# Attention steps of the next token chunk queued behind a feed-forward unit's last work on every engine

## The chip, the cores and the metric

One NeuronCore of one Trainium2 chip runs the whole program. The metric is device time in microseconds (us) of one execution; lower is better. Matmuls run on TensorE (PE in the rows, PEld its weight loads), elementwise work on VectorE (DVE), ScalarE (ACT) and GpSimd (POOL). All DMAs of this kernel are issued from the queue of SyncE (SP).

## What is computed

The reference runs a gated linear attention and feeds its output through two feed-forward networks:

```python
for t in range(S):                                   # S = 768, B = 4, H = 8, D = 48
    state = alpha[:, :, t, :, None] * state + einsum('bhd,bhe->bhde', k[:, :, t], v[:, :, t])
    y[:, :, t] = einsum('bhd,bhde->bhe', q[:, :, t], state)
x = y.transpose(0, 2, 1, 3).reshape(B * S, H * D)     # 3072 tokens x 384
h = x @ w_in                                          # 384 -> 2048
P = a[0] + a[1]*h + a[2]*h**2 + a[3]*h**3
Q = 1 + |b[0]|*|h| + |b[1]|*h**2
x2 = (P / (Q + 1e-6)) @ w_out                         # 2048 -> 384
h = x2 @ w_in2                                        # 384 -> 1024
out = layernorm(h * softmax(h)) * g_ln @ w_out2       # 1024 -> 384
```

## The kernel before, in words

**Chunks, units, halves.** The 768 time steps are cut into six chunks of 128 steps (4 x 128 = 512 tokens). The first feed-forward network handles a chunk in 16 *units*, one for each 128 columns of the 2048; `u` counts all 96 of them (`c, f = divmod(u, 16)`). A unit's up part, `m_up(u)`, is nine matmuls into the PSUM tile `hp` (L573; three such tiles take turns), then elementwise work on ACT (L578 to L581, L600, L601), DVE (L599, L602 to L604) and POOL, which ends with `fin[u]` (L604 or, for some early units, L597) on DVE, the copy `gh` (L606) on ACT and the remainder `gl` (L607) on POOL. Its down part, `m_down(u)`, is nine matmuls that add `gh` and `gl` into `x2p` (L619); it is written four units after the up part.

**Attention.** A chunk's attention is done in two *halves* (two of the four batches each), so there are 12; half `i` is prepared while the units of the chunk before are at work. `a_pe(i)` has four steps: for each of two groups of heads, `p` = 0 and 1, eight score products `sc` (L416, each recorded as two matmuls), their copies to `A` on ACT (L423) and a causal mask on POOL (L424); then 56 products into `y` (L437, 112 recorded), whose result goes into the next chunk's `xt` (L463 on ACT, L464 on DVE); then 16 products `u` (L474) and the update of the state `Sbd` (L484 on DVE, L485 on POOL, which multiplies by the decay of the whole chunk, `hf.ends`).

**Loading q and k.** `a_prep(i)` makes the scaled q, k and last decay products of a half on DVE and POOL and writes them out to DRAM (`qk_d`, L333; `kb_d`, L325). `a_move(i)`, run at the end of the half before, reads them back in another layout: four DMAs into `qks` (L276), which holds q, k and the last decay products, then v (`vns`, L344) and the k by time (`kns`, L278). `qks` is one buffer for all halves from 2 on, so its new content waits until the old is no longer read.

**What sets the order.** A scheduler orders each engine's instructions at build time, by when it reckons they are ready; at run time each engine takes them strictly in that order. The program can hold an instruction back: inside `with tc.issue_after(ins)` everything traced for the engine of `ins` is placed behind it. For the attention steps this is done by `half_steps`, one step at each unit from `u % 8 == 2` on:

```python
def later(n):
    return tc.issue_after(fin[now[0] - n].ins) if n <= now[0] < GE + n and now[0] - n in fin else ExitStack()
...
with later(GP):            # GP = 2
    a = next(gp, "end")    # a step of a_pe(i)
with later(GS):            # GS = 2
    b = next(gd, "end")    # two steps of a_prep(i + 1), then loads for half i + 2
```

As `fin` is on DVE, only DVE's part of a step is held back; PE, ACT and POOL take theirs where the scheduler reckons them ready.

**Side work.** While u < 16, units share the engines with the preparation of the first network's weights, later (u 16 to some 63) with that of the second's (`split_w`: load `st` L516, three DVE instructions L519 to L523, ACT L529, POOL L530, and a store L532). `judge` (L143) sums flags of a range check. The second network follows from unit 84 on.

Of the kernel before, what the change touches and what calls it, by code (L numbers as in the profile page):

```python
# [7 lines left out]
F32 = mybir.dt.float32  # L8
# [5 lines left out]
ALU = mybir.AluOpType  # L14
# [9 lines left out]
def _run(*gens):  # L24
    for g in gens:
        for _ in g:
            pass
# [3 lines left out]
def kernel(  # L31
# [108 lines left out]

    flag = const.tile([1, 1], I32, name="flag")

    def judge():  # L143

        sums = const.tile([128, 1], F32, name="sums")
        row = const.tile([1, 128], F32, name="row")
        tot = const.tile([1, 1], F32, name="tot")
        nc.vector.tensor_reduce(sums, bad, axis=AX.X, op=ALU.add)
        nc.sync.dma_start(out=row, in_=sums)
        nc.vector.tensor_reduce(tot, row, axis=AX.X, op=ALU.add)  # L150
        nc.vector.tensor_scalar(flag, tot, 0.0, None, ALU.is_gt)

    def network(fast):
# [116 lines left out]
                raws[i, nm] = t  # L270
                yield

        def a_move(i):
            qk, kb = moved.pop(i)
            for m, i0, n, d0 in ((0, 0, 32, 0), (1, 0, 16, 32), (1, 16, 16, 64), (2, 0, 32, 80)):
                nc.sync.dma_start(out=qks[d0:d0 + n], in_=qk[m].rearrange("b i x -> i b x")[i0:i0 + n])  # L276
            v_load(i)
            nc.sync.dma_start(  # L278
                out=kns[:, :B * 192].rearrange("p (b x) -> p b x", b=B), in_=kb[:].rearrange("b t x -> t b x")
            )  # L280
            yield
# [114 lines left out]
        def a_prep(i):  # L396
            if i >= NPE:
                yield from a_dve(i)
# [8 lines left out]
        def a_pe(i):  # L407
            c, bp = divmod(i, 2)
            vt = vts.pop(i)
            hf = half(i)  # L410
            A = {}
            for p in range(2):
                sc = [ps_ap.tile([128, B, CH], F32, name="sc", tag="at") for j in range(2)]
                for x in range(B):
                    for j in range(2):
                        nc.tensor.matmul(  # L416
                            sc[j][:, x, :],
                            lhsT=hf.k[p][64 * j:64 * j + D, x, :], rhs=hf.q[p][64 * j:64 * j + D, x, :],
                            start=True, stop=True,
                        )  # L420
                for j in range(2):
                    t = A[p, j] = ap_.tile([128, B, CH], F32, name="A", tag=f"A{p}{j}")
                    nc.scalar.activation(t, sc[j], AF.Copy)  # L423
                    nc.gpsimd.affine_select(  # L424
                        out=t, in_=t, pattern=[[0, B], [1, CH]], compare_op=ALU.is_ge, fill=0.0, base=0,
                        channel_multiplier=-1,
                    )
                yield

            y2 = [ps_ap.tile([128, n, 2 * CH], F32, name="y", tag="at") for n in (2, 1)]  # L430
            begun = set()

            def put(m, x, w, r, last):
                kt, quad = divmod(m, 4)
                first = (kt // 2, quad) not in begun
                begun.add((kt // 2, quad))
                nc.tensor.matmul(  # L437
                    y2[kt // 2][32 * quad:32 * quad + 32, kt % 2, CH * x:CH * x + CH], lhsT=w, rhs=r,
                    start=first, stop=last, skip_group_check=True,
                )  # L440

            pairs = range(H // 2)
            for x in range(2):
                if c:
                    for hp in pairs:
                        g, p = divmod(hp, 2)
                        for z in range(3):
                            put(
                                3 * hp + z, x, Sbd[:, bp, 2 * (2 * x + g) + p, 32 * z:32 * z + 32],
                                hf.q[p][:, 2 * x + g, :], False,  # L450
                            )
                for part in ((0, 1, 3), (2,)):
                    for hp in pairs:
                        g, p = divmod(hp, 2)
                        for z in part:
                            o = 512 * x + 128 * hp + (0, 32, 48, 80)[z]
                            put(
                                3 * hp + (0, 1, 1, 2)[z], x, vt[:, o:o + 32], A[p, z // 2][:, 2 * x + g, :], z != 1
                            )
            xt = x_tile(c)  # L460
            for z, n in enumerate((2, 1)):
                hi, lo = (xt[:, 2 * z:2 * z + n, w, 256 * bp:256 * bp + 256] for w in range(2))
                nc.scalar.activation(hi, y2[z], AF.Copy)  # L463
                marks[i, z] = nc.vector.tensor_tensor(lo, y2[z], hi.bitcast(F32), ALU.subtract)  # L464
            yield
            if i < NPE:
                a_back(i)
            u = ps_ap.tile([128, B * 2, D], F32, name="u", tag="at")
            for x in range(B):
                for p in range(2):  # L470
                    for j in range(2):
                        o = 192 * x + 96 * p + 48 * j
                        n = 256 * x + 128 * p + 64 * j
                        nc.tensor.matmul(  # L474
                            u[64 * j:64 * j + 64, 2 * x + p, :], lhsT=hf.kn[:, o:o + 64], rhs=vt[:, n:n + D],
                            start=True, stop=True, skip_group_check=True,
                        )
            if c < NCH - 1:
                for j in range(2):
                    rows = slice(64 * j, 64 * j + D)  # L480
                    S = Sbd[rows, bp, :, D * j:D * j + D]
                    S4 = S.rearrange("p (b w) e -> p b w e", b=B)
                    if c:
                        nc.vector.tensor_tensor(S, S, u[rows], ALU.add)  # L484
                        nc.gpsimd.tensor_tensor(S4, S4, hf.ends[rows], ALU.mult)  # L485
                    else:
                        nc.vector.tensor_tensor(
                            S4, u[rows].rearrange("p (b w) e -> p b w e", b=B), hf.ends[rows], ALU.mult
                        )
            yield  # L490

# [68 lines left out]
                )  # L560

        fin = {}
        gts = {}
        x2ps = {}

        def m_up(u):
# [3 lines left out]
            hi, lo = wi[n]  # L570
            for kt in range(KT):
                for w, xx in ((hi, 0), (hi, 1), (lo, 0)):
                    nc.tensor.matmul(  # L573
                        hp, lhsT=w[:, kt, 128 * o:128 * o + 128], rhs=xts[c][:, kt, xx, :],
                        start=(kt == 0 and w is hi and xx == 0), stop=(kt == KT - 1 and w is lo),
                    )
# [26 lines left out]
                nc.vector.scalar_tensor_tensor(hp, w, 2.0, hp, ALU.subtract, ALU.mult, reverse0=True)  # L603
                fin[u] = nc.vector.scalar_tensor_tensor(p, p, a0, hp, ALU.add, ALU.mult)  # L604
            gh, gl = (moe_pool.tile([128, NTOK], F32R, name=nm, tag=nm, bufs=NB[nm]) for nm in ("gh", "gl"))
            nc.scalar.activation(gh, p, AF.Copy)  # L606
            nc.gpsimd.tensor_tensor(gl, p, gh[:].bitcast(F32), ALU.subtract)  # L607
            gts[u] = (gh, gl)

        def m_down(u):  # L610
# [176 lines left out]
        if fast:  # L787
# [16 lines left out]
            _run(a_load(2, ("ra", "rk")))  # L804
            with tc.issue_after(marks[0, 1].ins):
                _run(a_prep(2))
            _run(a_enter(2), pre)
            _run(a_load(3, ("ra", "rk")))
            stage["wide"] = False
# [4 lines left out]
        NH = 2 * NCH  # L814

        now = [0]

        def later(n):
            return tc.issue_after(fin[now[0] - n].ins) if n <= now[0] < GE + n and now[0] - n in fin else ExitStack()

        def half_steps(i):
            gp = a_pe(i)
            gd = chain(a_prep(i + 1), a_load(i + 2, ("ra", "rk")) if i + 2 < NH and i + 1 >= NPE else iter(())) if i + 1 < NH else iter(())
            while True:
                with later(GP):
                    a = next(gp, "end")
                with later(GS):
                    b = next(gd, "end")
                    if b != "end":
                        b = next(gd, "end")  # L830
                if a == "end" and b == "end":
                    if i + 1 < NH:
                        _run(a_enter(i + 1))
                        if i + 2 < NH and i + 1 < NPE:
                            _run(a_load(i + 2))
                    return
                yield

        NU = NCH * NF1
        split2 = w2_split() if fast else iter(())  # L840
        tp = 0.0
        side = iter(())
# [2 lines left out]
        for u in range(NU + LAG):  # L845
# [6 lines left out]
            if u < NU:  # L852
                if f == 0 and c == NCH - 1:
                    if fast:
                        judge()
                    open2()
                    tail = chain(w2_load("i"), n_load(0), w2_load("o"))
                if f == 0 and c and not fast:
# [169 lines left out]
```

## Time and profile before

| | |
|---|---|
| three runs | 814.88, 815.14 and 816.88 us; median 815.14 us |
| the profiled execution | 812.64 us, of which the span from first to last instruction is 810.9 us |
| PE | busy 748.0 us (92%) |
| DVE | busy 634.7 us (78%) |
| ACT, POOL | busy 535.4 us (66%), 361.1 us (45%) |
| mean granted TensorE clock | 0.96 of full speed |

All times of rows are of the profiled execution, counted from the start of its span. In a unit's row of nine matmuls a recorded duration is longer than the distance to the next start, since matmuls overlap; the distances are what counts.

### The profile page before, as it was taken

The page shows a single profiled execution, that of the slowest core. Times are in us where ns is not written, and L with a number is a line of the kernel's source. Part 1 is how long each engine was busy: PE and PEld are TensorE (multiplying, and loading weights), DVE is VectorE, ACT ScalarE, POOL GpSimd, SP SyncE. Part 2 cuts the span into 40 slices and gives each one's busy share as a digit, 9 for nine tenths or more (in the row PEclk, how much of TensorE's full clock was granted, in tenths as well). Part 3 has the DMA queues.
Part 4 walks back from the last instruction along what each step waited for, and adds up shares of the span by engine and source line. Part 5 has one row for each costly group of instructions (what it writes and reads, how often), then busy time and mean ns, then how long its engine had stood idle before and what let it go on. Part 6 is the DMA issues. An engine that isn't in the chain of part 4 may idle for free. (4 is left out here: it accounts for less than half of the span.)

```text
span 810.9 us, 13869 instructions
## 1 busy us (share of the span) xinstructions
PE 748.0 (92%) x4976; PEld 614.9 (76%) x4976; DVE 634.7 (78%) x1110; ACT 535.4 (66%) x983; POOL 361.1 (45%) x294
## 2 busy tenths in 40 slices
PE   4776987999899998999899999999999999999995
PEld 4665776777676775878687777888888989998995
DVE  6996998979698987979798976557877698777720
ACT  2324766777786876687887878798885555555531
POOL 3263778676554453444444433242233514452331
PEclk9857698999999998999999999999999999999999
DMA  7877357355737275355636160460013544552552
GB/s 177 183 186 209 105 122 199 114 138 165 199 93 175 77 235 123 120 118 161 152 99 176 47 150 1 146 244 1 1 39 90 151 95 119 132 117 50 121 129 58
DMA packets 87279, 101.75 MB, mean 125 GB/s; under 512 B 34464, under 2 KB 63136, under 8 KB 87200
## 3 DMA queue, kind: packets, MB, share of 16 engines
q1 hardware_dynamic: 87200, 100.77, 47.0%
q8 instruction: 41, 0.67, 0.4%
q14 instruction: 38, 0.31, 0.1%
HBM read 60.59 MB, written 27.56 MB: 109 GB/s over the span
## 5 line engine op out<-in xcount | busy, mean ns | idle before, releaser
L573 PE MATMUL hp<-xt,g 128*128 128x512 f32 x864 | 225.8, 406 | 12.6 <-DVE p L604 7.4
L573 PEld LDWEIGHTS hp<-xt,g 128*128 128x128 f32 x864 | 163.4, 193 | 54.5 <-DVE p L604 11.3
L619 PE MATMUL x2p<-gh,g 128*128 128x512 f32 x576 | 196.9, 398 | 0.1
L607 POOL TENSOR_TENSOR gl<-p,gh 128x512 fp32r<-128x512 f32 x96 | 130.7, 1363 | 148.1 <-ACT gh L606 101.7
L619 PEld LDWEIGHTS x2p<-gh,g 128*128 128x128 f32 x576 | 108.5, 189 | 25.7 <-issue 1.0
L619 PE MATMUL x2p<-gl,g 128*128 128x512 f32 x288 | 115.0, 399 | 2.4 <-POOL gl L607 2.3
L757 PE MATMUL op<-w2oh,room 128*128 128x384 f32 x384 | 101.9, 339 | 0.5 <-ACT o L766 0.4
L749 POOL TENSOR_TENSOR room<-room,room 128x1024 fp32r<-128x1024 f32 x22 | 53.8, 2448 | 102.5 <-ACT room L748 74.6
L602 DVE SCALAR_TENSOR_TENSOR w<-w,co,hp 128x512 f32<-128x512 f32 x84 | 61.7, 736 | 41.9 <-ACT hp L601 41.6
L693 PE MATMUL h<-w2ih,x 128*128 128x512 f32 x288 | 90.7, 395 | 0.0
L599 DVE SCALAR_TENSOR_TENSOR p<-p,co,hp 128x512 f32<-128x512 f32 x84 | 61.9, 737 | 27.5 <-ACT p L580 26.9
L578 ACT ACTIVATE ah<-hp 128x512 f32<-128x512 f32 x96 | 56.6, 590 | 26.7 <-PE hp L573 26.2
L580 ACT ACTIVATE p<-hp,co 128x512 f32<-128x512 f32 x96 | 65.5, 682 | 9.9 <-POOL gl L607 9.6
L757 PEld LDWEIGHTS op<-w2oh,room 128*128 128x128 f32 x384 | 70.1, 188 | 2.1 <-ACT o L766 0.7
L581 ACT ACTIVATE w<-ah,co 128x512 f32<-128x512 f32 x96 | 69.2, 721 | 2.9 <-DVE hp L603 2.4
L601 ACT ACTIVATE hp<-ah 128x512 f32<-128x512 f32 x84 | 50.3, 599 | 29.8 <-DVE p L599 29.2
L619 PEld LDWEIGHTS x2p<-gl,g 128*128 128x128 f32 x288 | 54.6, 190 | 16.2 <-POOL gl L607 4.3
L757 PE MATMUL op<-w2ol,room 128*128 128x384 f32 x192 | 65.0, 339 | 0.0
L606 ACT ACTIVATE gh<-p 128x512 fp32r<-128x512 f32 x96 | 60.0, 625 | 7.4 <-PE x2p L619 5.0
L604 DVE SCALAR_TENSOR_TENSOR p<-p,co,hp 128x512 f32<-128x512 f32 x84 | 62.2, 740 | 1.0
L693 PEld LDWEIGHTS h<-w2ih,x 128*128 128x128 f32 x288 | 53.9, 188 | 11.7
L600 ACT ACTIVATE ah<-w,co 128x512 f32<-128x512 f32 x84 | 60.6, 721 | 1.0
(164 smaller groups left out, 1296.5 us busy)
## 6 DMA issues: line engine op xcount, KB each, us to landing
room<-room SPq DMA_DIRECT2D x96, 128.0 KB, 2.3
qk_d<-qk SPq DMA_DIRECT2D x10, 771.0 KB, 5.4
st<-in_moe_w_in_dram SPq DMA_DIRECT2D x15, 512.0 KB, 4.8
st<-in_moe_w_out_dram SPq DMA_DIRECT2D x20, 384.0 KB, 3.7
qks<-qk_d SPq DMA_DIRECT2D x20, 257.0 KB, 5.7
x<-x_d SPq DMA_DIRECT2D x18, 256.0 KB, 3.4
out_dram<-o SPq DMA_DIRECT2D x96, 48.0 KB, 1.6
ra<-in_alpha_dram SPq DMA_DIRECT2D x44, 96.0 KB, 3.2
```

The costliest lines, as they stand in the source:

```text
L573: nc.tensor.matmul(hp, lhsT=w[:, kt, 128 * o:128 * o + 128], rhs=xts[c][:, kt, xx, :], start=(kt == 0 and w is hi and xx == 0), stop=(kt = ...
L580: nc.scalar.activation(p, hp, AF.Square, bias=co[:, 7:8])
L581: nc.scalar.activation(w, ah, AF.Square, bias=co[:, 6:7])
L599: nc.vector.scalar_tensor_tensor(p, p, a1, hp, ALU.add, ALU.mult)
L600: nc.scalar.activation(ah, w, AF.Ln, bias=rest)
L602: nc.vector.scalar_tensor_tensor(w, w, rest, hp, ALU.add, ALU.mult)
L604: fin[u] = nc.vector.scalar_tensor_tensor(p, p, a0, hp, ALU.add, ALU.mult)
L606: nc.scalar.activation(gh, p, AF.Copy)
L607: nc.gpsimd.tensor_tensor(gl, p, gh[:].bitcast(F32), ALU.subtract)
L619: nc.tensor.matmul(x2ps[c][d], lhsT=w[:, o, 128 * d:128 * d + 128], rhs=gg, start=(f == 0 and w is hi and gg is gh), stop=(f == NF1 - 1 an ...
L693: nc.tensor.matmul(hp[:, 512 * n:512 * n + 512], lhsT=x2s[c][:, kt, x, CH * b:CH * b + CH], rhs=w2[w][:, kt, 512 * n:512 * n + 512], start ...
L757: nc.tensor.matmul(op, lhsT=x[:, 128 * f:128 * f + 128], rhs=w2[w][:, f, :], start=(f == 0 and x is hi and w == "oh"), stop=(f == NF2 - 1 ...
```

## The change

Four edits. (1) For the steps of `a_pe`, `later` gives way to `pin`: at unit u a step's PE instructions come behind the last up matmul of unit u, its ACT instructions behind `gh` of unit u - 2, its POOL instructions behind `gl` of unit u - 2, its DVE instructions behind `fin` of unit u - 2 as before. (2) The last decay products are copied from `qks` into a tile of their own, `end`, on POOL, ahead of the `y` products; the state update reads that. (3) The four `qks` DMAs leave `a_move` and become a step of their own, `a_move_qk`, which comes behind the preparation of the half, some two units earlier in the program. (4) `judge` puts a row of 128 numbers in a buffer of the unit pool.

```diff
-        row = const.tile([1, 128], F32, name="row")
+        row = moe_pool.tile([1, 128], F32, name="row", tag="ft", bufs=2)
...
-        def a_move(i):
-            qk, kb = moved.pop(i)
+        def a_move_qk(i):
+            qk, kb = moved[i]
             for m, i0, n, d0 in ((0, 0, 32, 0), (1, 0, 16, 32), (1, 16, 16, 64), (2, 0, 32, 80)):
                 nc.sync.dma_start(out=qks[d0:d0 + n], in_=qk[m].rearrange("b i x -> i b x")[i0:i0 + n])
+            yield
+
+        def a_move(i):
+            kb = moved.pop(i)[1]
             v_load(i)
...
+            end = ap_.tile([128, B, 2], F32, name="end", tag="end", bufs=2)
+            nc.gpsimd.tensor_copy(end, hf.ends[:, :, :, 0])
+            ends = _view(end[:], 0, [[2, B], [1, 2], [0, D]])
...
-                        nc.gpsimd.tensor_tensor(S4, S4, hf.ends[rows], ALU.mult)
+                        nc.gpsimd.tensor_tensor(S4, S4, ends[rows], ALU.mult)
...
+        def pin(n):
+            stack = ExitStack()
+            if n <= now[0] < NU and fast:
+                for e, u in (("PE", now[0]), ("ACT", now[0] - n), ("POOL", now[0] - n)):
+                    stack.enter_context(tc.issue_after(last[e, u].ins))
+                stack.enter_context(tc.issue_after(fin[now[0] - n].ins))
+            return stack
+
         def half_steps(i):
             gp = a_pe(i)
-            gd = chain(a_prep(i + 1), a_load(i + 2, ("ra", "rk")) if i + 2 < NH and i + 1 >= NPE else iter(())) if i + 1 < NH else iter(())
+            gd = chain(a_prep(i + 1), a_move_qk(i + 1) if i + 1 >= NPE else iter(()), a_load(i + 2, ("ra", "rk")) if i + 2 < NH and i + 1 >= NPE else iter(())) if i + 1 < NH else iter(())
             while True:
-                with later(GP):
+                with pin(GP):
                     a = next(gp, "end")
```

**PE's order at half 7.** In the program of before, TensorE meets the first score products of half 7 around the up part of units 40 and 41 (`hp`, weights `g_735`); `x2p` rows are down matmuls:

```order
L573 MATMUL hp<-xt,g_735 128x512 x9
L619 MATMUL x2p_2991<-gh,g_619 128x512
L619 MATMUL x2p_2992<-gh,g_619 128x512
L619 MATMUL x2p_2993<-gh,g_619 128x512
L416 MATMUL sc<-qks 128x128
L619 MATMUL x2p_2991<-gl,g_619 128x512
L619 MATMUL x2p_2991<-gh,g_619 128x512
L619 MATMUL x2p_2992<-gl,g_619 128x512
L619 MATMUL x2p_2992<-gh,g_619 128x512
L619 MATMUL x2p_2993<-gl,g_619 128x512
L619 MATMUL x2p_2993<-gh,g_619 128x512
L416 MATMUL sc<-qks 128x128 x2
```

The changed program, whose lines have other numbers (L581 is the up part, L627 the down part, L420 the scores), has them behind unit 42:

```order
L581 MATMUL hp<-xt,g_739 128x512 x9
L420 MATMUL sc<-qks 128x128 x8
L627 MATMUL x2p_3005<-gh,g_623 128x512
L627 MATMUL x2p_3005<-gl,g_623 128x512
L627 MATMUL x2p_3005<-gh,g_623 128x512
L627 MATMUL x2p_3006<-gh,g_623 128x512
L627 MATMUL x2p_3006<-gl,g_623 128x512
L627 MATMUL x2p_3006<-gh,g_623 128x512
L627 MATMUL x2p_3007<-gh,g_623 128x512
L627 MATMUL x2p_3007<-gl,g_623 128x512
L627 MATMUL x2p_3007<-gh,g_623 128x512
L581 MATMUL hp<-xt,g_739 128x512 x9
```

The first eight score products of this half stood in four pieces (1, 2, 2 and 3) from unit 40 on; they now stand in one piece behind the up part of unit 42, two units later. For halves 4 to 11 the number of pieces of these eight goes from 2, 2, 3, 4, 4, 3, 3 and 4 to one each; the second eight are one piece before and after.

**SP's order at half 7.** The DMA queue of SyncE in the program of before, from the write of half 7's q and k (`qk_d`) to its last `qks` load; `st` are loads, `w2i_d` and `w2o_d` stores of the weight preparation:

```order
L333 DMA qk_d<-qk 128x3x514
L516 DMA st<-in_moe_w_out_dram 128x384
L532 DMA w2i_d<-st 256x1x512
L516 DMA st<-in_moe_w_out_dram 128x384
L344 DMA vns<-in_v_dram 128x8x48 x2
L278 DMA kns<-kb_d 128x4x192
L276 DMA qks<-qk_d 32x4x514
L276 DMA qks<-qk_d 16x4x514
L532 DMA w2o_d<-st 256x1x384
L276 DMA qks<-qk_d 16x4x514
L276 DMA qks<-qk_d 32x4x514
```

And of the change (L337 is the write, L523 a weight load, L539 a store):

```order
L337 DMA qk_d<-qk 128x3x514
L539 DMA w2i_d<-st 256x1x512
L276 DMA qks<-qk_d 32x4x514
L276 DMA qks<-qk_d 16x4x514 x2
L276 DMA qks<-qk_d 32x4x514
L523 DMA st<-in_moe_w_out_dram 128x384
L348 DMA vns<-in_v_dram 128x8x48
L539 DMA w2o_d<-st 256x1x384
L348 DMA vns<-in_v_dram 128x8x48
L282 DMA kns<-kb_d 128x4x192
```

The four `qks` loads moved ahead of `vns` and `kns`, which wait for the `u` products, and ahead of two weight loads `st`.

## Rows read from the trace of the kernel before

**Rows 1.** The page: busy time and share of the span; the clock in 40 slices.

```profile
PE 748.0 (92%) x4976; PEld 614.9 (76%) x4976; DVE 634.7 (78%) x1110; ACT 535.4 (66%) x983; POOL 361.1 (45%) x294
PEclk9857698999999998999999999999999999999999
```

**Rows 2.** Busy us of each engine in three stretches (stretch, length, engines, clock, DMA).

```profile
81.00:171.10 90.10, 81.41 (x578) 64.03 (x579) 86.66 (x141) 63.05 (x116) 68.74 (x56) 0.89 0.50 134
171.10:530.00 358.90, 341.70 (x2577) 267.94 (x2577) 293.69 (x471) 279.54 (x502) 161.51 (x140) 0.99 0.50 134
530.00:811.00 281.00, 271.63 (x1309) 238.78 (x1307) 190.15 (x353) 166.00 (x309) 99.40 (x58) 0.99 0.35 93
```

**Rows 3.** Waits of PE from 171 to 530 us: us in total, times, longest.

```profile
PE sc L416 <- DMA qks<-qk_d: 8.3, 5, 3.8
PE hp L573 <- DVE p L604: 4.3, 6, 1.4
PE x2p L619 <- POOL gl L607: 2.3, 4, 0.9
```

**Rows 4.** Busy us around 310 us, stretches as in Rows 2.

```profile
304.00:309.10 5.10, 2.83 (x12) 1.99 (x12) 3.17 (x5) 4.60 (x9) 2.06 (x2) 1.00 1.09 216
309.10:315.90 6.80, 5.24 (x14) 3.65 (x15) 4.34 (x8) 3.76 (x7) 1.31 (x2) 0.50 0.41 99
315.90:322.70 6.80, 6.80 (x35) 5.07 (x34) 5.45 (x10) 4.23 (x9) 2.78 (x3) 1.00 0.16 52
```

**Rows 5.** Timeline of SP's queue, 284 to 312 us: start, us, what.

```profile
290.56 0.43 SPq L333 DMA_DIRECT2D qk_d<-qk  x1
...
302.07 1.03 SPq L276 DMA_DIRECT2D qks<-qk_d  x2
...
303.97 1.00 SPq L276 DMA_DIRECT2D qks<-qk_d  x2
```

**Rows 6.** Timeline of POOL, same half.

```profile
303.11 0.84 POOL L485 TENSOR_TENSOR Sbd<-Sbd,qks 48x384 f32<-48x384 f32 x1
```

**Rows 7.** Timeline of PE, same half: end of the y products, the u products.

```profile
286.55 1.13 PE L437 MATMUL y<-A,vns 128*32 128x128 f32 x31
...
294.31 1.14 PE L474 MATMUL u<-vns,kns 128*64 128x48 f32 x32 [0.48 <-DVE xt L464]
```

**Rows 8.** The page's DMA issues: KB each, median us to landing.

```profile
qk_d<-qk SPq DMA_DIRECT2D x10, 771.0 KB, 5.4
```

**Rows 9.** Timeline of PE, half 8: a piece of four score matmuls, one of sixteen.

```profile
358.32 0.40 PE L619 MATMUL x2p<-gh,g 128*128 128x512 f32 x1
358.65 0.49 PE L416 MATMUL sc<-qks 48*128 48x128 f32 x4
359.07 2.34 PE L573 MATMUL hp<-xt,g 128*128 128x512 f32 x9
361.25 0.39 PE L619 MATMUL x2p<-gh,g 128*128 128x512 f32 x1
...
372.06 0.39 PE L619 MATMUL x2p<-gh,g 128*128 128x512 f32 x1
372.38 1.49 PE L416 MATMUL sc<-qks 48*128 48x128 f32 x16
373.79 0.50 PE L619 MATMUL x2p<-gh,g 128*128 128x512 f32 x1
374.13 0.39 PE L619 MATMUL x2p<-gl,g 128*128 128x512 f32 x1
374.36 0.39 PE L619 MATMUL x2p<-gh,g 128*128 128x512 f32 x1
```

**Rows 10.** Timeline of ACT, half 8, second group: the copies of the scores.

```profile
375.18 1.09 ACT L423 ACTIVATE A<-sc 128x512 f32<-128x512 f32 x2
```

**Rows 11.** Timeline of POOL, half 8, second group: the masks.

```profile
375.86 1.22 POOL L424 TENSOR_SCALAR_AFFINE_SELECT A<-A 128x512 f32<-128x512 f32 x2 [4.35 <-ACT A L423]
```

**Rows 12.** Waits of DVE from 60 to 171 us, the longest.

```profile
DVE ft L519 <- DMA lent<-in_moe_w_out_dram: 7.2, 2, 5.8
```

More of the change, by code (lines that the diff above doesn't have):

```diff
@@ L141, with judge @@
     flag = const.tile([1, 1], I32, name="flag")
-    def judge():
+    def judge(moe_pool):
         sums = const.tile([128, 1], F32, name="sums")
-        row = const.tile([1, 128], F32, name="row")
+        row = moe_pool.tile([1, 128], F32, name="row", tag="ft", bufs=2)
         tot = const.tile([1, 1], F32, name="tot")
@@ L484, in a_pe @@
                         nc.vector.tensor_tensor(S, S, u[rows], ALU.add)
-                        nc.gpsimd.tensor_tensor(S4, S4, hf.ends[rows], ALU.mult)
+                        nc.gpsimd.tensor_tensor(S4, S4, ends[rows], ALU.mult)
                     else:
                         nc.vector.tensor_tensor(
-                            S4, u[rows].rearrange("p (b w) e -> p b w e", b=B), hf.ends[rows], ALU.mult
+                            S4, u[rows].rearrange("p (b w) e -> p b w e", b=B), ends[rows], ALU.mult
                         )
@@ L562, in network @@
         fin = {}
+        last = {}
         gts = {}
@@ L572, in m_up @@
                 for w, xx in ((hi, 0), (hi, 1), (lo, 0)):
-                    nc.tensor.matmul(
+                    last["PE", u] = nc.tensor.matmul(
                         hp, lhsT=w[:, kt, 128 * o:128 * o + 128], rhs=xts[c][:, kt, xx, :],
@@ L605, in m_up @@
             gh, gl = (moe_pool.tile([128, NTOK], F32R, name=nm, tag=nm, bufs=NB[nm]) for nm in ("gh", "gl"))
-            nc.scalar.activation(gh, p, AF.Copy)
-            nc.gpsimd.tensor_tensor(gl, p, gh[:].bitcast(F32), ALU.subtract)
+            last["ACT", u] = nc.scalar.activation(gh, p, AF.Copy)
+            last["POOL", u] = nc.gpsimd.tensor_tensor(gl, p, gh[:].bitcast(F32), ALU.subtract)
             gts[u] = (gh, gl)
@@ L806, in network @@
                 _run(a_prep(2))
+            _run(a_move_qk(2))
             _run(a_enter(2), pre)
@@ L816, in network @@
         now = [0]
+        NU = NCH * NF1
         def later(n):
             return tc.issue_after(fin[now[0] - n].ins) if n <= now[0] < GE + n and now[0] - n in fin else ExitStack()
+        def pin(n):
[5 more added lines that the diff above has]
+            return stack
         def half_steps(i):
             gp = a_pe(i)
-            gd = chain(a_prep(i + 1), a_load(i + 2, ("ra", "rk")) if i + 2 < NH and i + 1 >= NPE else iter(())) if i + 1 < NH else iter(())
+            gd = chain(a_prep(i + 1), a_move_qk(i + 1) if i + 1 >= NPE else iter(()), a_load(i + 2, ("ra", "rk")) if i + 2 < NH and i + 1 >= NPE else iter(())) if i + 1 < NH else iter(())
             while True:
-                with later(GP):
+                with pin(GP):
                     a = next(gp, "end")
-                with later(GS):
+                with pin(GS):
                     b = next(gd, "end")
@@ L837, in half_steps @@
                 yield
-        NU = NCH * NF1
         split2 = w2_split() if fast else iter(())
@@ L854, in network @@
                     if fast:
-                        judge()
+                        judge(moe_pool)
                     open2()
```

## Prediction, made before the changed kernel had run

> **What bounds the kernel now.** I read the busy shares of the page first, then the busy time by stage, then TensorE's waits in the stage that the change touches. TensorE (PE) is busy 92% of the span and no other engine over 78%; its clock falls in the first quarter and once more in the second [rows 1]. The stages differ [rows 2]. From 81 to 171 us DVE is busy 86.66 of 90.10 us: there DVE sets the pace, and a wait of PE that goes away comes back as another, up to DVE's own idle time of 3.4 us. From 171 to 530 us PE is busy 341.70 of 358.90 us and DVE 293.69 (82%): PE sets the pace, and 17.2 us of it are idle. From 530 us on the second network runs, and no instruction of it changes in kind or number.
>
> In the middle stage PE's longest wait is that of the score products for the DMAs into `qks`: 8.3 us in five waits, one of them 3.8 us [rows 3]. What follows is in the rows around 310 us: PE is busy 2.83 of 5.10 us, the granted clock then drops to 0.50 (1.2 in place of 2.4 GHz) for 6.8 us, and is back at 1.00 [rows 4].
>
> Why `qks` is late is seen at half 7. The `y` products of half 6 end at 287.7 us [rows 7] and nothing reads the old q and k after that; `qk_d` is issued at 290.56 us. But the `qks` loads go out at 302.07 and 303.97 us, two each [rows 5]: the last pair right after POOL's second multiply of `Sbd` ends at 303.95 us [rows 6], as that multiply reads the decay products at the end of `qks`, and it follows the `u` products of 294.31 us [rows 7]. PE, whose order has the first score product right behind unit 40, stands until 310.66 us.
>
> **The change part by part.**
>
> *Waits on qks.* In the changed program `qks` is free after the `y` products and a small POOL copy, and its loads stand right behind `qk_d` in SP's queue. They then wait for the landing of `qk_d`: 290.56 plus 5.4 us [rows 8] is 296 us, against 304 us for the last pair now: 8 us earlier. And PE asks for them two units later (behind unit 42 in place of unit 40); the nine up and nine down matmuls of a unit, 0.23 us apart (the last two starts of rows 9), are 4.1 us, so this is 8 us more. Sixteen us of margin against a longest wait of 3.8 us: all five waits go. Minus 8.3 us.
>
> *Clock.* The drop follows the idle stretch at 304 to 310 us, in which this wait was the longest. During it PE did 5.24 us of work at half speed [rows 4], which takes 2.6 us at full speed. Minus 2.6 us; bounds 0 (the clock falls elsewhere) and 3.4 us (all of the 6.8).
>
> *Pieces.* A piece of score matmuls between feed-forward matmuls costs more than its own work [rows 9]. Four of them: from 358.32 to 361.25 us are 2.93 us, less ten other matmuls at 0.23 us leaves 0.63. Sixteen: from 372.06 to 374.36 us are 2.30 us, less three at 0.23 leaves 1.61. So a matmul costs (1.61 - 0.63) / 12 = 0.08 us and a piece, however short, 0.30 us. For halves 4 to 11, which lie in the PE-bound stage, the first eight products stand in 25 pieces before and in 8 after, by the order: 17 x 0.30 = 5.1 us. Bounds: 0, if a piece only fills time in which PE would have waited for DVE; 17 x 0.63 = 10.7, if the dear piece is the rule. I take 5.1, as pieces are spread over units in which PE ran without idle time.
>
> *Where DVE sets the pace.* Halves 2 and 3 lose their waits too, but the stage gives at most DVE's 3.4 us of idle time [rows 2], and may give nothing. I take 1.0.
>
> *POOL copies.* Twelve copies of eight columns a partition are added, ten of them beside units. Nothing of this size and kind stands in the trace; the nearest row is the multiply of 384 columns, 0.84 us [rows 6], so between 0 and 10 x 0.84 = 8.4 us of POOL, which is busy 45% [rows 1]. On the path: 0. The Trainium skill, page "SBUF — State Buffer", section "SBUF: two separate sides", says that a GpSimd instruction and a DVE instruction with two SBUF inputs shut each other out for the whole of an instruction; by it the estimate would be up to 8.4 us of DVE time, so 797 to 805 us in place of 797, if all of it reached PE. No row here shows such a copy, and the sum goes without it.
>
> *Waits that the pins add.* Queued behind `gh` and `gl` of unit u - 2, copies and masks of a group can come late for the `y` products. In half 8 the second group's scores end at 373.8 us [rows 9], the copies start at 375.18 [rows 10], the masks end at 377.08 [rows 11]: 3.3 us. In the changed order some 22 feed-forward matmuls stand between those scores and `y`, 22 x 0.23 = 5.1 us. That leaves 1.8 us of margin, and DVE's lag behind PE (4.3 us of waits for a free `hp`, 2.3 us for `gl` [rows 3]) may grow when PE runs faster. I put 1.5 us against the gain; bounds 0 and what the rivals make of it.
>
> *Nothing.* `judge`'s row in another buffer costs nothing where `ft` is not in use, behind the last weight split; uncovered it would be one DMA, once.
>
> The sum, against the profiled execution of 812.64 us (span 810.9 and 1.7 around it): 812.64 - 8.3 - 2.6 - 5.1 - 1.0 + 1.5 = 797.1 us. The median of the runs, 815.14, lies 2.5 us above that execution, so I forecast 799.5 us.
>
> **The rivals.**
>
> *DVE takes over.* If DVE cannot be kept busier than the 82% that it has in the middle stage, because it waits for ACT within each unit, PE's gains of 16.0 us return as waits for a free `hp`. Only the last units, in which no weights are split, keep theirs: I put that at a third of the pieces and of nothing else, 1.7 us, and 5 us in all with one or two waits that were pure loss. That gives 810 us. For it speaks the 4.3 us that PE waits for `p` even now; against it that DVE runs at 96% from 81 to 171 us [rows 2], so 82% is no ceiling. At a gain of 16 us DVE would be at 293.69 / 342.9 = 86%.
>
> *The masks come late.* If ACT or POOL runs 2 us further behind than in half 8, `y` waits 0.2 us a half; at 4 us it waits 2.2 us, in eight halves 17.6 us, and the gain is gone: 815 us. For it: every ACT and POOL instruction of a step is now last in line. Against: the pinned neighbours (`gh`, `gl` of unit u - 2) must be done before PE may start the up part of unit u + 1 anyway, or nearly, since three `hp` tiles take turns.
>
> *Weight loads stuck in SP's queue (slower).* The `qks` loads wait at the head of SP's queue for `qk_d` to land, 5.4 us [rows 8], and take 2.0 us to issue [rows 5]; behind them now stand loads `st` that stood ahead of them. DVE takes its instructions in order and stops at a load that isn't there: that cost it 5.8 us in one place [rows 12]. In five halves a load stands there. If each reaches PE whole, 5 x 7.4 = 37 us, against a gain of 17: 815 + 20 = 835 us. It decides from 3.4 us a half on. Against it: two `st` buffers take turns, so a load is mostly issued a whole split ahead of its use, and PE has up to three units of `hp` before it feels DVE.
>
> *The change doesn't do what it says.* PE's order and SP's order have moved as told, so only the wait itself could remain, if landing took 16 us more: out of the question beside a median of 5.4.
>
> **How the numbers follow.** A measurement of this kernel tells some 0.3% (2.4 us) from no change. Chances: the forecast 0.72, its own range 791 to 806 (from 0 to 10.7 us for the pieces and 0 to 8 us of new waits); DVE takes over 0.12 at 810; masks late 0.08 at 815; weight loads stuck 0.08 at 818 to 835. The range 789 to 811 us holds the first two. Faster: the first two and a little of the third, 0.85; same 0.08; slower 0.07.
>
> **What would show it.** In the changed profile PE waits for `qks` nowhere from 171 to 530 us; the clock is at 1.00 from 300 to 330 us; score matmuls stand in runs of sixteen; the `qks` loads are issued some 8 us after the `y` products end, ahead of the second `Sbd` multiply; from 530 us to the end the profile is as long as before. DVE's busy share in the middle stage is about 86%. I would be wrong if PE waits for `p` (DVE) grow by 8 us or more, if `y` waits for POOL or ACT more than 1 us a half, or if DVE's L519 waits for DMAs in the middle stage.

## The result, and the profile after

The changed kernel took 807.01 us (median of five runs, 804.24 to 809.60; before, five runs beside it, median 814.88). The ratio is 0.991, with a 95% interval of 0.989 to 0.994; a second series of twelve, beside other runs of before, gave 806.51 us and 0.994 (0.991 to 0.997). One of the twelve, of 815.60 us, was slow; the ratio and the means below leave it out, and without it the median is 805.81 us. So it is faster, by about 0.75%, inside the range that was given, but with a gain of 6 to 8 us where 15.6 were forecast. The profiled execution took 805.28 us (span 803.5, before 810.9). Its page, as in [rows 1]:

```profile
PE 736.9 (92%) x4976; PEld 613.0 (76%) x4976; DVE 641.5 (80%) x1110; ACT 535.4 (67%) x983; POOL 365.4 (45%) x306
PEclk9757797999999998999999999999999999999998
```

PE is busy 11 us less with the same 4976 instructions, DVE 7 us more with the same 1110. To see where, the span is cut at units, by the first up matmul of unit 0, 16 and 80. These are the stretches from 60 us to unit 16, then to unit 80, then (after only) to the end; the columns are those of [rows 2]. First the kernel before:

```profile
60.00:171.10 111.10, 95.92 (x661) 75.33 (x662) 100.09 (x161) 72.18 (x134) 76.42 (x64) 0.86 0.55 149
171.10:524.50 353.40, 336.20 (x2553) 263.38 (x2553) 290.11 (x467) 274.84 (x495) 159.74 (x138) 0.99 0.49 130
```

Then the changed kernel:

```profile
60.00:177.30 117.30, 92.17 (x660) 72.12 (x661) 104.07 (x160) 72.35 (x134) 75.75 (x64) 0.87 0.55 151
177.30:517.70 340.40, 327.95 (x2553) 263.32 (x2552) 293.24 (x469) 275.56 (x497) 165.49 (x148) 0.98 0.49 130
517.70:803.50 285.80, 276.88 (x1333) 243.35 (x1331) 193.09 (x358) 170.99 (x317) 101.36 (x59) 0.99 0.38 103
```

The PE-bound stage, units 16 to 80, became 13.0 us shorter, and the first 16 units, where DVE sets the pace, 6.2 us longer (with what precedes them). The remainder is 0.6 us shorter. In the middle stage PE's busy time fell by 8.3 us. Its waits there are these two alone (us in total, times, longest), to be held against [rows 3]:

```profile
PE hp L581 <- DVE p L612: 7.9, 8, 3.0
PE u L481 <- DVE xt L471: 4.4, 4, 1.5
```

No wait on `qks` is left. The place of [rows 5, 7] shows why: in half 7 the last `y` products start at 289.64 us and end a microsecond later, the `qks` loads go out at 300.99 us, and PE asks for them at 319.26 us. Timeline of PE, then of SP's queue (start, us, what):

```profile
289.64 1.06 PE L444 MATMUL y<-A,vns 128*32 128x128 f32 x32
...
319.26 1.16 PE L420 MATMUL sc<-qks 48*128 48x128 f32 x16
```

```profile
292.67 0.43 SPq L337 DMA_DIRECT2D qk_d<-qk  x1
...
300.99 2.41 SPq L276 DMA_DIRECT2D qks<-qk_d  x4
```

But the clock still falls close by, as in [rows 4]. Busy us of three stretches, and of a fourth, earlier one:

```profile
295.00:300.90 5.90, 2.93 (x14) 2.11 (x13) 4.96 (x9) 2.25 (x5) 1.27 (x1) 1.00 0.58 190
300.90:307.70 6.80, 6.72 (x44) 5.14 (x43) 5.66 (x11) 5.73 (x11) 3.55 (x4) 0.50 0.96 203
307.70:315.00 7.30, 7.30 (x33) 5.96 (x32) 6.09 (x11) 6.61 (x11) 3.46 (x4) 0.99 0.98 260
...
208.80:212.20 3.40, 3.40 (x8) 2.72 (x9) 3.27 (x5) 1.89 (x4) 2.19 (x2) 0.50 0.73 208
```

PE is busy for half of the 5.9 us ahead (it stands 3.0 us for DVE's `p` at unit 39), and then runs 6.8 us at 1.2 GHz. The last line is a second drop in the middle stage, behind a wait of PE for `p` of 1.90 us; the kernel before has one there, that of [rows 4].

```profile
208.74 5.08 PE L581 MATMUL hp<-xt,g 128*128 128x512 f32 x14 [1.90 <-DVE p L612]
```

### The profile page after: what moved, and what is told of

The parts are those of the page before. It is cut to its first block, busy times and chain, and to the rows that moved or that the text cites. A ratio compares the mean times of both kernels' runs of the same rounds, so it can differ in the third digit from the quotient of the medians.

```text
span 803.5 us, 13909 instructions
## 1 busy us (share of the span) xinstructions
PE 736.9 (92%) x4976; PEld 613.0 (76%) x4976; DVE 641.5 (80%) x1110; ACT 535.4 (67%) x983; POOL 365.4 (45%) x306
## 5 line engine op out<-in xcount | busy, mean ns | idle before, releaser
L581 PE MATMUL hp<-xt,g 128*128 128x512 f32 x864 | 229.7, 408 | 24.9 <-DVE p L612 20.8
L581 PEld LDWEIGHTS hp<-xt,g 128*128 128x128 f32 x864 | 165.3, 195 | 68.0 <-DVE p L612 26.9
L627 PE MATMUL x2p<-gh,g 128*128 128x512 f32 x576 | 196.3, 397 | 0.0
L627 PEld LDWEIGHTS x2p<-gh,g 128*128 128x128 f32 x576 | 109.2, 190 | 25.4 <-issue 0.6
L627 PE MATMUL x2p<-gl,g 128*128 128x512 f32 x288 | 113.2, 393 | 0.4 <-POOL gl L615 0.4
L765 PE MATMUL op<-w2oh,room 128*128 128x384 f32 x384 | 101.6, 339 | 0.2 <-DVEq L1012 0.2
L757 POOL TENSOR_TENSOR room<-room,room 128x1024 fp32r<-128x1024 f32 x22 | 54.2, 2469 | 102.8 <-ACT room L756 87.8
L627 PEld LDWEIGHTS x2p<-gl,g 128*128 128x128 f32 x288 | 54.3, 189 | 12.6 <-POOL gl L615 0.8
```

Of the source, the lines that this page charges most:

```text
L581: last["PE", u] = nc.tensor.matmul(hp, lhsT=w[:, kt, 128 * o:128 * o + 128], rhs=xts[c][:, kt, xx, :], start=(kt == 0 and w is hi and xx = ...
L627: nc.tensor.matmul(x2ps[c][d], lhsT=w[:, o, 128 * d:128 * d + 128], rhs=gg, start=(f == 0 and w is hi and gg is gh), stop=(f == NF1 - 1 an ...
L765: nc.tensor.matmul(op, lhsT=x[:, 128 * f:128 * f + 128], rhs=w2[w][:, f, :], start=(f == 0 and x is hi and w == "oh"), stop=(f == NF2 - 1 ...
```

## Experiments

Each was timed in five rounds beside the kernel before (on the same chip within one group; its median there was 812.3 to 812.7 us), but for the second profile of before, which is one execution. "Unit 16" is the start of that unit's first up matmul in the profiled execution, "middle" the time from there to unit 80; starts are rounded to 0.1 us before they are subtracted. "Pins" are more than the list of the change says: `with later(GS)` became `with pin(GS)` too, so the steps that prepare the next half (`a_prep` and the `qks` loads) also come behind the unit's work on PE, ACT and POOL. All rows with pins have both; "no pins on `a_pe`" has the pins of the preparation alone, and "from unit 16 on" drops both before that unit.

| kernel | us | ratio (95% interval) | unit 0 to 14 | unit 0 to 16 | middle |
|---|---|---|---|---|---|
| before, first profile | 814.88 | 1 | 101.6 | 111.2 | 353.4 |
| before, second profile | 812.54 | | 101.0 | 113.3 | 348.0 |
| changed | 807.01 | 0.991 (0.989 to 0.994) | 105.6 | 115.7 | 340.4 |
| changed, again | 806.51 | 0.994 (0.991 to 0.997) | 105.1 | 115.3 | 340.2 |
| pins from unit 16 on | 803.96 | 0.990 (0.987 to 0.994) | 102.8 | 113.8 | 342.0 |
| loads and copies, no pins on `a_pe` | 825.58 | 1.017 (1.014 to 1.021) | 101.4 | 112.6 | 361.4 |
| pins and copies, loads late | 805.34 | 0.991 (0.988 to 0.994) | 105.6 | 115.7 | 339.0 |
| pin on PE alone, with copies | 835.52 | 1.029 (1.026 to 1.033) | 107.6 | 115.5 | 368.3 |
| pins only | 806.81 | 0.992 (0.988 to 0.995) | 105.5 | 115.6 | 342.9 |
| pins only, from unit 16 on | 802.28 | 0.988 (0.984 to 0.991) | 101.4 | 111.0 | 341.2 |
| the same, again | 801.41 | 0.989 (0.985 to 0.992) | 101.5 | 111.1 | 341.1 |
| copies alone | 828.10 | 1.020 (1.016 to 1.023) | 101.2 | 110.8 | 366.0 |
| pin on PE alone, no copies | 816.86 | 1.006 (1.003 to 1.009) | 106.6 | 116.7 | 351.6 |
| ACT and POOL pinned from unit 16 on, PE everywhere | 803.57 | 0.991 (0.988 to 0.994) | 105.5 | 113.3 | 338.6 |

The theory at the outset: the middle stage gained about as forecast, and the pins lose half of it in the first 16 units. Its rivals: the loads or the POOL copies lose it; or it is only lent.

**Pins from unit 16 on.**

```diff
         def pin(n):
             stack = ExitStack()
+            if now[0] < NF1:
+                return later(n)
```

> The pins act only from unit 16 on; before it the steps stand as in the kernel before; everything else as in the changed kernel. Theory (the pins cost the DVE-bound first 16 units some 6 us, and the loads, pieces and pins give some 13 us in units 16 to 80): unit 16 starts at 171 to 173 us in place of 177.3, and the time is 801 to 803 us. Rival A (the early loss comes from the qks loads and the end copies, not from the pins): unit 16 still starts at 176 to 178 us and the time stays at 806 to 808. Rival C (what is lost early is only lent, and would be lost later anyway because DVE sets the pace over the whole of units 0 to 80): unit 16 earlier, but units 16 to 80 longer by as much, 806 to 808 us.

Unit 16 started at 175.2 us, between the two bounds, and the median of 803.96 us fell just outside the theory's. That nothing was given back (middle 342.0) spoke against the third view; the rest stayed open.

**Loads and copies without the pins on `a_pe`.**

```diff
-                with pin(GP):
+                with later(GP):
                     a = next(gp, "end")
```

> The pin on the steps of the PE part of a half (scores, masks, y, u) is taken back to the old rule, which orders them behind DVE's last work of a unit alone; the end copies, the early qks loads and the row tile stay. Theory: the score products stand in short pieces again, so the gain of the pieces (5 to 11 us in units 16 to 80) is gone, the waits on qks stay away (8 us), and the early loss of 6 us is gone too: unit 16 at 171 to 173 us, units 16 to 80 in 344 to 348 us, time 806 to 809 us. Rival A (the early loss comes from the loads and copies): unit 16 at 176 to 178 us and a time of 811 to 814 us.

Neither: 825.58 us, slower than before by 1.7%. Earlier loads did not even end the waits on `qks`: PE asks for them as early as before (half 7 in unit 40), and there the last went out at 312.0 us, with the first product at 320.7. Waits of PE in the middle stage, the longest:

```profile
PE sc L420 <- DMA qks<-qk_d: 8.7, 5, 3.9
```

**Pins and copies, the loads back where they were.**

```diff
         def a_move(i):
-            kb = moved.pop(i)[1]
+            kb = moved[i][1]
+            _run(a_move_qk(i))
+            moved.pop(i)
...
-gd = chain(a_prep(i + 1), a_move_qk(i + 1) if i + 1 >= NPE else iter(()), ...
+gd = chain(a_prep(i + 1), ...
```

> The pins and the end copies stay, the qks loads go back to where they were, issued when a half is entered. Theory: the scores are asked for two units later by the pins and by then the loads have mostly landed, so at most 3 us of waits on qks come back: 807 to 810 us, and unit 16 at 176 to 178 us as in the changed kernel. Rival A (the early loss comes from the early loads): unit 16 at 171 to 173 us, and a time of 801 to 805 us. Rival D (the early loads are needed for the 8.3 us): waits on qks of 6 us or more and a time of 813 to 816 us.

805.34 us, no wait on `qks` in the middle stage, unit 16 at 177.7 us. The early loads neither bring the gain nor cost the start.

**The pin on PE alone, with the copies.**

```diff
-for e, u in (("PE", now[0]), ("ACT", now[0] - n), ("POOL", now[0] - n)):
+for e, u in (("PE", now[0]),):
```

> The steps are queued behind the unit's work on PE and, as before, behind DVE's last work of the unit two back, but no longer behind gh on ACT and gl on POOL. If the early loss and the waits on DVE (p, xt) come from ACT and POOL work of a step being held back, unit 16 starts at 171 to 173 us, the waits of PE on p and xt from 177 to 530 us fall below 8 us from 12.3, and the time is 799 to 803 us. If it is the hold on PE that sets the early order (the scores of a group in one piece ahead of which PE runs a unit further), unit 16 starts at 176 to 178 us and the time is 806 to 809 us.

Neither again: 835.52 us, the slowest of all. PE's longest wait in the middle stage, and POOL's on the loads:

```profile
PE x2p L627 <- POOL gl L615: 15.3, 7, 4.5
```

```profile
POOL end L434 <- DMA qks<-qk_d: 34.5, 8, 8.2
```

One place, the timeline of POOL and then of PE, shows how the two hang together:

```profile
316.08 0.19 POOL L434 COPY end<-qks 128x8 f32<-128x8 f32 x1 [3.17 <-DMA qks<-qk_d]
316.23 1.26 POOL L615 TENSOR_TENSOR gl<-p,gh 128x512 fp32r<-128x512 f32 x1
```

```profile
317.54 0.80 PE L627 MATMUL x2p<-gl,g 128*128 128x512 f32 x1 [4.46 <-POOL gl L615]
```

The copy takes 0.19 us, but it reads `qks` of the next half. Unpinned, it stands on POOL ahead of a unit's `gl` and holds it until the load has landed; PE waits 4.46 us for that `gl`. In the changed kernel the pin on POOL puts the copy behind `gl`.

**Copies alone**, in the kernel before, with the row tile:

```diff
+            end = ap_.tile([128, B, 2], F32, name="end", tag="end", bufs=2)
+            nc.gpsimd.tensor_copy(end, hf.ends[:, :, :, 0])
+            ends = _view(end[:], 0, [[2, B], [1, 2], [0, D]])
...
-nc.gpsimd.tensor_tensor(S4, S4, hf.ends[rows], ALU.mult)
+nc.gpsimd.tensor_tensor(S4, S4, ends[rows], ALU.mult)
```

> The kernel before, with the POOL copies of the decay products into a tile of their own, and nothing else of the change but the row tile. If the copies (or the collisions of DVE with them) cost the start: unit 0 at 61.2 to 62.0 us, unit 16 at 173 to 175 us, and the time 2 to 4 us above the kernel before. If they cost nothing: unit 16 at 170.5 to 172 us and the time within 2 us of the kernel before.

828.10 us, 15 us above before: twelve instructions of 0.2 to 0.6 us. Unit 16 stayed at 172.2 us, so the start is not where they cost. The same rows as above, PE's and then POOL's, from the middle stage:

```profile
PE x2p L623 <- POOL gl L611: 10.2, 8, 2.5
PE u L478 <- DVE xt L468: 6.0, 4, 2.7
PE sc L416 <- DMA qks<-qk_d: 5.8, 4, 2.5
```

```profile
POOL end L431 <- DMA qks<-qk_d: 39.5, 8, 8.4
```

**The pin on PE alone, no copies** (the edits of "pins only" below and of "pin on PE alone"):

> The pin on PE alone, with no POOL copies and no early loads: beside the kernel in which PE alone was held and the copies stayed (832 us in its profile), only the copies go. Theory (there the copy of the next half stood on POOL ahead of gl and waited 34.5 us for the qks loads): PE's wait on gl falls from 15.3 us to below 4, and the time is 8 to 20 us below that kernel's ratio of 1.029, so 800 to 820 us. Rival (masks, too, stand ahead of gl on an unpinned POOL, and it is they that make gl late): the wait on gl stays at 8 us or more, and the time above 822 us.

816.86 us, and the wait on `gl` is 2.2 us. The early loads went together with the copies; but copies alone, with the loads late, have that wait too (10.2 us), so the copy made it. But the middle stage of 351.6 us lies where before's two do. The waits on `qks` are gone, and others stand in their place:

```profile
PE u L480 <- DVE xt L470: 5.7, 4, 2.6
PE x2p L626 <- ACT gh L613: 4.6, 3, 2.5
PE hp L580 <- DVE p L611: 3.7, 6, 1.1
```

So the pins on ACT and POOL, of the attention steps and the preparation together, are worth some 10 us here (351.6 against 339 to 343, and 816.86 against the 806.81 of the next kernel); the prediction booked them as a cost.

**Pins only**: late loads as above, no copies:

```diff
-            end = ap_.tile([128, B, 2], F32, name="end", tag="end", bufs=2)
-            nc.gpsimd.tensor_copy(end, hf.ends[:, :, :, 0])
-            ends = _view(end[:], 0, [[2, B], [1, 2], [0, D]])
...
-nc.gpsimd.tensor_tensor(S4, S4, ends[rows], ALU.mult)
+nc.gpsimd.tensor_tensor(S4, S4, hf.ends[rows], ALU.mult)
```

> Of the change only the pins are left: the decay products are read where they were, at the end of qks (no POOL copy), and the qks loads go out where a half is entered. Theory (the pins move the scores two units away from the loads, and that alone ends the waits on qks): waits on qks of at most 4 us from 177 to 530 us, and a time 6 to 10 us below the kernel before of the same session. If the POOL copies had cost DVE time, unit 16 comes 1 to 3 us earlier than in the changed kernel. Rival (copy and early loads are needed): waits on qks come back with 6 us or more, and the time is within 3 us of the kernel before.

806.81 us, 5.9 below before, with no wait on `qks` in the middle stage and unit 16 at 177.8 us. The pins by themselves do all that the change does, and lose the start as well.

**Pins only, from unit 16 on** (with the two lines of the first experiment):

> As the kernel with the pins alone, but the pins act only from unit 16 on; no POOL copies, no early loads. Up to unit 16 this is the kernel before. Theory (the loss ahead of unit 16 is made of the copies and of the pins there, half each): unit 16 starts at 171 to 172.5 us, units 16 to 80 take 339 to 342 us, and the time is 11 to 14 us below the kernel before. Rival (the profile of the kernel before was one of its faster starts, and the loss is spread between executions): unit 16 at 173 to 176 us here too, and the time is 7 to 10 us below the kernel before.

802.28 us and unit 16 at 172.0 us. Compared with "pins only", timed beside it, it is 4.1 us faster, plus or minus 2.4 (means of six runs each, 95%). The "half each" of the theory was wrong: the copies have no part in it.

**ACT and POOL pinned from unit 16 on, PE everywhere**:

```diff
-for e, u in (("PE", now[0]), ("ACT", now[0] - n), ("POOL", now[0] - n)):
+for e, u in (("PE", now[0]), ("ACT", now[0] - n), ("POOL", now[0] - n))[:1 if now[0] < NF1 else 3]:
```

> The pins on all engines from unit 16 on; before it PE alone is held; no copies, no early loads. It stands between the kernel with the pins everywhere (unit 16 at 177.8 us) and that with pins only from unit 16 on (172.0 us). If the hold on ACT and POOL costs the first 16 units their 4 to 5 us (POOL work falls beside DVE's weight splits): unit 16 at 171 to 173.5 us and a time of 801 to 803 us. If the hold on PE does it (the score products in one piece, PE's units further on): unit 16 at 176 to 178.5 us and 805 to 808 us.

803.57 us, unit 16 at 175.0 us: between the bounds. The three kernels with PE alone pinned in the start take 113.3, 115.5 and 116.7 us from unit 0 to 16, the seven with no pin on `a_pe` there 110.8 to 113.8, the four with all pins 115.3 to 115.7. At unit 14 the three are at 105.5 to 107.6 us, as late as the four with all pins (105.1 to 105.6). The hold on PE is enough for a part of the loss; how much the others add is not settled.

**The changed kernel and the best version, side by side.**

> The changed kernel once more, beside the next one on the same chip: 804 to 809 us, unit 16 at 176 to 178.5 us.

> The pins alone and only from unit 16 on, once more: 3 to 6 us below the changed kernel of the same call if the pins ahead of unit 16 cost what the profiles show (115.7 us against 111.0 from unit 0 to unit 16); within 2 us of it if that is the spread of the profiles.

806.51 against 801.41 us; the means of six and eleven runs are 4.8 us apart, plus or minus 3.3. The pins ahead of unit 16 cost 4 to 5 us, and without them the pins alone are faster than both kernels, by some 10 us than before.

**The kernel before, a second profile.**

> The kernel before once more, for a second profile. If its start is as steady as that of the five kernels that carry the copies (unit 0 at 61.2 to 62.0 us in all five), unit 0 starts at 59.5 to 60.3 us and unit 16 at 170 to 172 us. If executions differ by as much as the loss that is to be explained, unit 0 is above 61 us and unit 16 above 173 us.

Unit 0 at 60.4 us and unit 16 at 173.7 us, at or past the edge of steady. Its span of 810.8 us is that of the first profile, but its middle stage is 5.4 us shorter. There PE waits for `qks` 4.6 us, not 8.3 [rows 3], and the clock of the stage is 1.00. The waits of PE and the busy time:

```profile
PE sc L416 <- DMA qks<-qk_d: 4.6, 4, 2.0
```

```profile
60.00:173.70 113.70, 95.32 (x662) 74.59 (x663) 101.71 (x162) 74.58 (x137) 78.80 (x65) 0.86 0.56 154
173.70:521.70 348.00, 334.47 (x2552) 261.94 (x2551) 289.23 (x464) 272.68 (x493) 157.76 (x137) 1.00 0.49 130
```

## Why the prediction was right and wrong

The direction was right, and the margin by which PE asks later held: no wait on `qks`. The sum missed by 8.2 us (797.1 forecast for the profiled execution, 805.28 measured). By stage: 7.2 us of that up to unit 16, 1.5 in the middle, minus 0.6 after. That the middle came so close is luck in part: of its terms the pieces gave twice the forecast, and clock and new waits took that back.

- **Where DVE sets the pace (minus 1.0): this is the step that failed.** I let the stage give at most DVE's idle time and lose nothing. It lost 2 to 4.5 us from unit 0 to 16 (115.7 and 115.3 against 111.2 and 113.3); against the best version, whose start is unpinned, 4 to 5 us, which the times show as well. DVE fills that stage [rows 2], and I priced the pins' new order only for PE. Where DVE has done as many instructions in either order, at unit 14 (147 and 146), the distance is plainest: 101.0 to 102.8 us in the seven profiles without pins on `a_pe` there, 105.1 to 105.6 in the four with all. The rows of this stretch are below: here DVE's busy time makes 3.7 of the 4.0 us; on the means of the seven and the four it makes 2.4 of 3.9 us (91.7 to 94.2), and its idle time the other 1.5. So its instructions grew longer and it stood longer. Why stays open; the last section says what is known. The 1.7 us by which unit 0 came later are spread: the changed kernel's second profile has unit 0 at 60.1 us.

  From unit 0 to unit 14, busy us; the kernel before, the changed one, and the best version:

```profile
59.90:161.50 101.60, 86.45 (x593) 67.63 (x593) 90.88 (x147) 65.15 (x121) 68.38 (x56) 0.85 0.54 149
```

```profile
61.60:167.20 105.60, 82.77 (x593) 64.51 (x593) 94.55 (x146) 63.05 (x117) 67.71 (x58) 0.85 0.52 144
```

```profile
59.70:161.20 101.50, 84.83 (x593) 66.13 (x593) 90.86 (x147) 65.24 (x121) 66.48 (x56) 0.87 0.55 150
```

- **Waits on qks (minus 8.3)**: gone as forecast, with one of the two reasons given. The pins do it, by PE asking two units later; the early loads add nothing that these runs can tell. The size was that of one execution; another of the same kernel has 4.6 us.
- **Clock (minus 2.6): failed.** I tied the drop at 309 us to one wait. Without that wait it came at 300.9 us and once more at 208.8 us, behind waits on DVE, at a cost of 5.1 us (half of 6.72 and 3.40 us of PE work): 2.5 more than before, not 2.6 less. Before's second profile has the waits and no drop in the middle stage; the changed kernel's second has two, of 3.4 us of PE work each. This term should have been nothing, with a bound on either side.
- **Pieces (minus 5.1)**: half of what they gave. PE's busy time in the middle fell by 8.3 us, in the second pair of profiles from 334.47 to 327.36, by 7.1. With the work at half speed counted at full speed it fell from 333.6 to 322.9, by 10.7, and in the second pair from 334.5 to 324.0, by 10.5: the upper bound. The count was right, 33 runs of score products in the middle stage before and 16 after, 17 fewer; the price was not, 0.62 us each, as the dear piece of [rows 9] has it (0.63), and not 0.30. That it is the pieces rests on all fourteen profiles: the four with 28 or 33 runs have 332.9 to 334.5 us of such work, the ten with 16 or 17, all pinned on PE, have 322.9 to 326.5; pieces were not joined without the pin.
- **POOL copies (nothing)**: right beside the pins, though by luck. I bounded them by their duration, and what an unpinned copy costs is where it stands: 15 us, with 0.2 us a copy. The bound of 8.4 us did not hold that.
- **Waits that the pins add (plus 1.5)**: 4.0. PE waited for DVE (`p`, `xt`) and `gl` 8.3 us before and 12.3 after.

Of the rivals, "DVE takes over" was true for the first 16 units and not for the middle, where DVE's share is 293.24 of 340.40 us, 86%, as forecast. The masks did not come late for `y` (0.3 us, once, ahead of unit 16). Weight loads did not stick: DVE's waits on `st` in the middle stage are 3.8 us against 1.4 before, and 4.5 with the pins only, where the loads are late.

## What to carry to other kernels

A block of work is better held back on all its engines than on one: here that made 0.992 of the time before, and PE alone 1.006. An instruction that waits for a DMA should not stand ahead of work that others need: twelve copies, most of 0.2 us, cost 15 us. Ask stage by stage whether to hold back: the same pins gave some 10 us where PE sets the pace and lost 4 to 5 where DVE does, though the two stages differ in more than that. And take a wait's size from more than one execution before it becomes a term: two profiles of one kernel, equal in length, differed by half in the wait and by a clock drop.

## What the runs showed that was not expected

DVE's weight-split instruction, which reads two SBUF operands, is stretched beside some POOL work. From unit 0 to 16 of seven profiles (before, changed, pins only and pins only from unit 16 on, all but the third twice), 75 of them had no POOL instruction beside them and took at most 0.68 us; the 44 that began during a `gl` took 1.18 us on the mean, and the 14 that began during POOL's `w` with a single tensor operand 0.64 us, all but two of them at most 0.72. From the changed kernel, DVE's row and POOL's:

```profile
91.64 0.68 DVE L529 SCALAR_TENSOR_TENSOR ft<-st,ft 128x512 int32<-128x512 int32 x1
92.23 1.75 DVE L530 SCALAR_TENSOR_TENSOR ft<-st,ft 128x512 int32<-128x512 int32 x1
```

```profile
91.72 1.72 POOL L615 TENSOR_TENSOR gl<-p,gh 128x512 fp32r<-128x512 f32 x1 [0.23 <-ACT gh L614]
```

The second DVE instruction of 128 x 512 starts inside `gl` and takes 1.75 us; it ends 0.5 us behind `gl`. The Trainium skill, page "SBUF — State Buffer", section "SBUF: two separate sides", says that DVE instructions with two SBUF inputs and GpSimd instructions that read SBUF exclude each other for a whole instruction. The row agrees; the 14 of 0.64 us do not fit it as it stands.

This does not explain the loss at the start, though. From unit 0 to unit 14 these instructions take 0.85 us each with and without the pins: 25.6 us for 30 on the mean of the seven profiles without pins on `a_pe` there, 26.5 us for 31 on that of the four with all. What grew is the first instruction of a split, with one SBUF operand (16 of them, 9.9 to 11.3 us), and the scan that makes the decay products (two, 4.1 to 5.2 us). The first scan is the clearest: it takes 2.73 us in all four with the pins, where it starts just behind a POOL instruction, and 1.76 in six of the seven without. DVE's row and POOL's, changed kernel, then DVE's of before:

```profile
98.17 2.73 DVE L308 TENSOR_TENSOR_SCAN P<-alT,d 128x774 f32<-128x774 f32 x1
```

```profile
97.99 1.29 POOL L537 TENSOR_TENSOR g<-ft,g 128x512 fp32r<-128x512 f32 x1
```

```profile
95.22 1.76 DVE L304 TENSOR_TENSOR_SCAN P<-alT,d 128x774 f32<-128x774 f32 x1
```

So the order sets which POOL work falls beside which DVE work, and the pins moved it. But the kernel with pins on the preparation alone has both scans at 2.8 us and more, and reaches unit 14 after 101.4 us, with six DVE instructions fewer done. The cause of the 4 to 5 us is not shown.
